# Where half range checks and one chunk's finish stand in the order of a gated-attention and SoLU kernel

## The chip, the cores and the metric

The kernel runs on one core of a Trainium2 chip. Its time is the device time of one execution in microseconds (us). Before the change three runs gave a median of 378.04 us (377.9 to 379.68). The core has five engines with a queue each: TensorE (PE, matrix products), VectorE (DVE), ScalarE (ACT), GpSimd (POOL) and SyncE (SP, which here only issues transfers). An engine works through its own queue in order; between engines there are only semaphores.

## The reference

Two blocks in a row. The first is a gated linear recurrence over 768 steps for 4 batches, 8 heads and a head width of 48; the second is a feed-forward layer on its 3072 rows of 384.

```
state = alpha[:, :, t, :, None] * state + einsum('bhd,bhe->bhde', k[:, :, t], v[:, :, t])
y[:, :, t] = einsum('bhd,bhde->bhe', q[:, :, t], state)
...
h = x @ w_in                                  # 384 -> 1024
e = exp(h - max(h));  solu = h * e / (sum(e) + 1e-9)
ln = (solu - mean(solu)) / sqrt(var(solu) + 1e-6) * g_ln
out = ln @ w_out                              # 1024 -> 384
```

The weights arrive as 64-bit floats, the rest as 32-bit.

## The kernel before

**Tiling.** Time is cut into six groups g of 128 steps; a group has the 4 batches side by side, so 512 rows at once. A chunk n = 4g + b is one batch of one group, 128 rows of the output. Attention for a group is done in closed form: products of alpha run along time (DVE scans, L204), keys and queries are scaled by them, `scores` makes key-by-query products on PE in two halves of the heads, `masked` (L289, DVE) takes the part at or before the diagonal into sT, `read_state` and `read_values` make y on PE, ACT copies y to x, and `next_state` with `decay` (L261, POOL) carries the state to the next group.

**Feed-forward.** For each group there are eight ups f, one per 128 of the 1024 hidden columns. `up_mm` (L388) makes h in one of two psum buffers. `up_act` then does three steps on two engines: exponential on ACT (L402), u = h times it on DVE (L403), and the square of u on ACT (L404). The buffer of h is free when L403 has read it. For group 0 the exponential and the square go to sT, which has four places: up f uses place f % 4. `array_sums` adds the exponentials and squares over the hidden columns on PE ("quarters", L431), in a first half at up 4 and a second half after the loop, and ACT copies them (L438). `down(n, half)` (L499) multiplies u by four of the eight blocks of w_out for one chunk. `finish(n)` (L524 to L541) brings a chunk to its end: three small DVE operations, a centring one for group 0 (L533), a power on POOL (L538), a scaling on ACT (L540) and the store on SP. `hold` (L508) copies a chunk out of psum, for chunks 0 and 1.

**Weights.** The 64-bit weights come in eight pieces, 0 to 3 of w_in and 4 to 7 of w_out. `fetch` brings a piece (or two) to a slot of `room`. `bits(i, part)` converts it on DVE: part 0 is L599 and L602, part 1 is L607, L610 and L611, and without a part it does both. `in_range(i)` checks on ACT that the magnitudes can be held: a square with a sum (L587), then an exponential of it with a sum (L588). `scaled(i)` (L618, ACT) multiplies a piece of w_out by the gain. `mean` (L632 to L640) takes the mean over w_out's rows once all eight pieces are there.

**What sets the order.** The program's order is each engine's order (`tc.manual_schedule()`): nothing moves work about. The loop `for f in range(FC)` over group 0's eight ups is written out by hand, with conversions, checks, fetches and loads between the ups. The transfers named here are issued by SP in that same order, so one that waits holds all behind it. `ends_k` and `ends_q` are ACT copies of parts of the next group's k and q; they wait for those loads (`load_first`, issued at up 0). After the loop, group 1's keys and queries are made while group 0's downs run.

Of the kernel before, what the change touches and what calls it, by code (L numbers as in the profile page):

```python
# [9 lines left out]
FP = mybir.dt.float32  # L10
# [3 lines left out]
AF = mybir.ActivationFunctionType  # L14
ALU = mybir.AluOpType
AX = mybir.AxisListType
P = 128
# [15 lines left out]
def fast_path(ctx, tc, q, k, v, alpha, moe_w_in, moe_w_out, moe_g_ln, out):  # L33
# [12 lines left out]
    nc = tc.nc  # L46
# [15 lines left out]
    def pool(name, bufs, **kw):  # L62
        return ctx.enter_context(tc.tile_pool(name=name, bufs=bufs, **kw))
# [6 lines left out]
    one = pool("one", 1)  # L70
# [215 lines left out]
    def masked(half, batches=range(B)):  # L286
        a = masks[half]
        for b in batches:
            nc.vector.tensor_tensor(  # L289
                out=sT[:, b, half * NP : half * NP + NP], in0=a[b], in1=mask[:, None, :].to_broadcast([P, NP, P]),  # L290
                op=ALU.mult,
            )
# [25 lines left out]
    parts = []  # L318
# [58 lines left out]
    def u_of(g, f):  # L377
        return slots[((0, 5, 4), (1, 2, 3))[g % 2][f // 3]][:, T4 * (f % 3) : T4 * (f % 3) + T4]
# [12 lines left out]
            )  # L391
        d["h"] = h

    def up_act(g, f):
        d = gr[g]
        h = d["h"]
        if g:
            e, u2 = (ring.tile([P, T4], FP, name=x) for x in ("e", "u2"))
        else:
            e, u2 = (sT[:, f % 4, 4 * i : 4 * i + 4].rearrange("p b t -> p (b t)") for i in range(2))  # L400
        u = u_of(g, f)
        nc.scalar.activation(out=e, in_=h, func=AF.Exp)  # L402
        nc.vector.tensor_tensor(out=u, in0=h, in1=e, op=ALU.mult)  # L403
        nc.scalar.activation(out=u2, in_=u, func=AF.Square)  # L404
        d[f] = e, u2

# [15 lines left out]
    def array_sums(g, half):  # L422


        d = gr[g]
        if half == 0:
            d["q"] = [ps_a.tile([P, T4], FP, tag=f"a{i}", name=f"quarters{i}") for i in range(2)]
        for i in range(2):
            for f in range(4):
                r = quarter(f)  # L430
                nc.tensor.matmul(  # L431
                    d["q"][i][r], lhsT=ones[:, 0:32], rhs=d[4 * half + f][i], start=half == 0, stop=half == 1,
                    tile_position=(0, r.start), skip_group_check=True,
                )
        if half:
            d["p"] = one.tile([P, 2, T4], FP, name="p")
            for i in range(2):
                nc.scalar.copy(out=d["p"][:, i], in_=d["q"][i])  # L438
            d["unit"] = small_ones
# [53 lines left out]
    def down(n, half, part=range(HF)):  # L493
        g, b = divmod(n, B)
        d = st[n]
        if half == 0 and 0 in part:
            d["o"] = ps_o.tile([P, 512], FP, tag="o", name="o")
        for f in (half * HF + i for i in part):
            nc.tensor.matmul(  # L499
                d["o"][:, 0 : DM + 1], lhsT=u_of(g, f)[:, b * P : b * P + P], rhs=w_out[:, f], start=(f == 0),  # L500
                stop=(f == FC - 1), skip_group_check=True,
            )
# [7 lines left out]
    def finish(n):  # L510
        g, b = divmod(n, B)
        d = st[n]
        s, whole = sums[:, n], d.get("held", d["o"])
        o = whole[:, 0:DM]
        t0 = b * S + g * P
        if g == G - 1:
            o_sb = work.tile([P, DM], FP, name="o_sb")
            r = gr[g]["r"][:, b : b + 1]
            nc.vector.tensor_scalar(out=o_sb[:, 0:P], in0=o[:, 0:P], scalar1=r, scalar2=None, op0=ALU.mult)  # L519
            nc.scalar.activation(out=o_sb[:, P:DM], in_=o[:, P:DM], func=AF.Copy, scale=r)  # L520
            nc.scalar.dma_start(out=out[t0 : t0 + P, :], in_=o_sb)
            d.clear()
            return
        nc.vector.tensor_copy(out=s[:, 0:1], in_=whole[:, DM : DM + 1])  # L524
        t = small.tile([P, 1], FP, name="t")
        nc.vector.scalar_tensor_tensor(
            out=t, in0=s[:, 0:1], scalar=-1.0 / DFF, in1=s[:, 0:1], op0=ALU.mult, op1=ALU.mult
        )
        nc.vector.tensor_tensor(out=s[:, 3:4], in0=t, in1=gr[g]["s"][:, b : b + 1], op=ALU.add)  # L529
        if g == 0:  # L530

            centred = work.tile([P, DM], FP, name="o_mean")
            nc.vector.scalar_tensor_tensor(  # L533
                out=centred, in0=mean_sb, scalar=s[:, 0:1], in1=o, op0=ALU.mult, op1=ALU.add
            )
            o = centred
        r = small.tile([P, 1], FP, name="r")
        nc.gpsimd.tensor_tensor(out=r, in0=s[:, 3:4], in1=mhalf, op=ALU.pow)  # L538
        o_sb = work.tile([P, DM], FP, name="o_sb")
        nc.scalar.activation(out=o_sb, in_=o, func=AF.Copy, scale=r)  # L540
        nc.sync.dma_start(out=out[t0 : t0 + P, :], in_=o_sb)  # L541
        d.clear()
# [8 lines left out]
    F = 2 * DM  # L551
# [5 lines left out]
    raws = {}  # L557
# [19 lines left out]
    far = const.tile([P, len(pieces), 2], FP, name="far")  # L577
    made = {}

    def in_range(i):  # L580


        if not float64:
            return
        hi = raws[i][:, :, :, 1].bitcast(FP)
        sq = one.tile([P, F], FP, name="sq").rearrange("p (c f) -> p c f", c=hi.shape[1])
        nc.scalar.activation(out=sq, in_=hi, func=AF.Square, accum_out=far[:, i, 0:1])  # L587
        nc.scalar.activation(out=sq, in_=sq, func=AF.Exp, scale=-(2.0**24), accum_out=far[:, i, 1:2])  # L588

    def bits(i, part=None):  # L590
        if not float64:
            return
        lo, hi = raws[i][:, :, :, 0], raws[i][:, :, :, 1]
        if part != 1:
            made[i] = [
                lots[2 * (i % 2) + x].rearrange("p (c f) -> p c f", c=hi.shape[1]) for x in range(2)
            ]
            top = made[i][0].bitcast(U32)
            nc.vector.tensor_scalar(  # L599
                out=top, in0=hi, scalar1=3, scalar2=0x3FFFFFF8, op0=ALU.logical_shift_left, op1=ALU.bitwise_and  # L600
            )
            nc.vector.scalar_tensor_tensor(  # L602
                out=top, in0=hi, scalar=0xC0000000, in1=top, op0=ALU.bitwise_and, op1=ALU.bitwise_or
            )
        if part != 0:
            top, low = made.pop(i)
            nc.vector.tensor_scalar(  # L607
                out=low.bitcast(U32), in0=top.bitcast(U32), scalar1=0xFF800000, scalar2=None, op0=ALU.bitwise_and
            )
            nc.vector.scalar_tensor_tensor(out=low, in0=lo, scalar=2.0**-52, in1=low, op0=ALU.mult, op1=ALU.mult)  # L610
            nc.vector.tensor_tensor(out=place(i), in0=low, in1=top, op=ALU.add)  # L611

    def scaled(i):

        f = pieces[i][1]
        for c in range(f, f + 2):
            w = w_out[:, c, 0:DM]
            nc.scalar.mul(out=w, in_=w, mul=g_col[:, c : c + 1])  # L618
# [78 lines left out]
    for i in (0, 2, 1):  # L697
        if i == 1:
# [3 lines left out]
            out=qe[:, :, 0:P] if i == 2 else qv[:, part, 0:P], in0=t[i], in1=aT[:, part, 1:SW], op=ALU.mult  # L702
# [17 lines left out]
    for f in range(FC):  # L720
        up_mm(0, f)
        if f == 4:
            array_sums(0, 0)
        up_act(0, f)

        for half in (0, 1) if f == 0 else (f + 1,):
            bits(2 + half // 2, half % 2)
        if f == 0:
            next_state(0)
            fetch(4, 3)  # L730
            load_first(k, kn, 1)
            load_first(q, qn, 1)
            load(alpha, an, 1)
        elif f == 1:
            in_range(2)
        elif f == 2:
            ends_k = ends_of(kn, "e")
        elif f == 3:
            in_range(3)
            fetch(5, 1)  # L740
            fetch(6, 2)
            ends_q = ends_of(qn, "u2")
        elif f == 5:
            in_range(4)
            fetch(7, 3)
            load_v(1)
        elif f == 6:
            scaled(4)
        elif f == 7:
            scaled(5)  # L750
    bits(6, 1)
    tk = three("tp_k", [(ps_a, "a2"), (ps_a, "a3"), (ps_h, "h")])
    turned(kn, ends_k, tk)
    load(k, kn, 2)
    array_sums(0, 1)
    down(0, 0)
    scaled(6)
    bits(7)
# [37 lines left out]
    scores(1, 0)  # L796
    decay(1)
    masked(0)
    finish(0)
    alpha_T(2)  # L800
    down(2, 1)
    scores(1, 1)
    masked(1)
    finish(1)
    finish(2)
    down(3, 0)
# [94 lines left out]
    for g in range(1, G + 1):  # L901
# [10 lines left out]
        for s in range(FC):  # L912
# [16 lines left out]
            if todo:  # L929
                n, half = todo.pop(0)  # L930
# [18 lines left out]
    parts = [N * 3, G * 2, G * NB] + [len(pieces)] * 2  # L949
# [5 lines left out]
    def compare(out, x, bound, op):  # L955
# [6 lines left out]
        out=chunks[:, :, 2], in0=sums[:, :, 2], scalar=0.25, in1=sums[:, :, 3], op0=ALU.mult, op1=ALU.is_le  # L962
# [6 lines left out]
    else:  # L969
# [9 lines left out]
        out=bad, in0=all_ok[0:1, 0:1], scalar1=float(P * ends[-1]), scalar2=None, op0=ALU.is_lt  # L979
# [451 lines left out]
```

## Time and profile before

| | |
|---|---|
| median of 3 runs | 378.04 us |
| the profiled execution's own time | 378.17 us |
| its span, first to last instruction | 376.4 us |
| PE busy | 362.0 us (96%) |
| DVE busy | 247.5 us (66%) |
| ACT busy | 145.8 us (39%) |
| POOL busy | 122.2 us (32%) |
| granted TensorE clock | 1.000 |

The profile is one execution. A timeline line gives the start and the length in us, the engine, the line of the kernel, the operation, what is written from what, the tile's shape and how many instructions were merged into it (an fp32 product of PE counts as two); in brackets stands how long the engine was idle before it and what ended that. Starts are from the span's first instruction. The span is shorter than the execution's time by what lies around it.

### The profile page before, as it was taken

The numbers are of one execution on the slowest core, as the hardware profiler recorded it, in microseconds if no ns is written. First come the engines' busy times: TensorE is split into PE (matmuls) and PEld (weight loads), VectorE is DVE, ScalarE is ACT, GpSimd is POOL, SyncE is SP. The second block draws the span as 40 slices with busy tenths as digits, with TensorE's granted clock in tenths as the row PEclk, the third lists the DMA queues.
The fourth block names the chain that finished last, engine by engine and source line by source line (L and its number), as shares of the span: only waits on it lengthen the run. The fifth ranks groups of instructions, "written<-read, shape, count | busy, mean of one in ns | idle before, by whom it ended". The sixth has DMA issues, their size and how long they took to land. (4 is left out here: it accounts for less than half of the span.)

```text
span 376.4 us, 10028 instructions
## 1 busy us (share of the span) xinstructions
PE 362.0 (96%) x4341; PEld 214.9 (57%) x4341; DVE 247.5 (66%) x377; ACT 145.8 (39%) x258; POOL 122.2 (32%) x127
## 2 busy tenths in 40 slices
PE   8989899999999999999999999999999999999994
PEld 7775335656655665556565556575556565555652
DVE  1999878997989979855756954756955314544500
ACT  3628566680365353352432351532241241332101
POOL 7000000000357992665112664112683211333200
PEclk9999999999999999999999999999999999999999
DMA  9983968239249616645034454004051000000011
GB/s 181 177 331 96 213 199 210 44 86 189 74 96 198 154 30 130 124 114 127 23 85 94 97 123 116 24 3 107 3 121 34 23 23 0 23 22 21 25 44 50
DMA packets 72439, 36.06 MB, mean 96 GB/s; under 512 B 48184, under 2 KB 69952, under 8 KB 72384
## 3 DMA queue, kind: packets, MB, share of 16 engines
q1 hardware_dynamic: 71360, 34.39, 38.8%
q10 hardware_dynamic: 1024, 0.92, 0.7%
q8 instruction: 36, 0.59, 0.7%
q14 instruction: 19, 0.16, 0.1%
HBM read 25.30 MB, written 4.72 MB: 80 GB/s over the span
## 5 line engine op out<-in xcount | busy, mean ns | idle before, releaser
L388 PE MATMUL h<-x,w_in 128*128 128x512 f32 x288 | 133.1, 601 | 3.1 <-DVE room L403 1.7
L499 PE MATMUL o<-w_out,room 128*128 128x385 f32 x384 | 133.6, 492 | 0.0
L499 PEld LDWEIGHTS o<-w_out,room 128*128 128x128 f32 x384 | 71.2, 190 | 54.5 <-issue 13.8
L388 PEld LDWEIGHTS h<-x,w_in 128*128 128x128 f32 x288 | 52.6, 190 | 61.9 <-issue 47.9
L403 DVE TENSOR_TENSOR room<-h,e 128x512 f32<-128x512 f32 x40 | 27.6, 690 | 60.8 <-ACT e L402 60.8
L402 ACT ACTIVATE e<-h 128x512 f32<-128x512 f32 x40 | 23.8, 596 | 95.2 <-PE h L388 92.6
L419 POOL TENSOR_TENSOR p<-p,e 128x512 f32<-128x512 f32 x30 | 42.9, 1429 | 27.3 <-ACT e L402 27.0
L404 ACT ACTIVATE u<-room 128x512 f32<-128x512 f32 x40 | 25.2, 630 | 36.5 <-DVE room L403 36.5
L538 POOL TENSOR_TENSOR r<-sums,mhalf 128x1 f32<-128x1 f32 x20 | 12.2, 610 | 73.7 <-DVE sums L529 73.6
L289 DVE TENSOR_TENSOR sT<-a,mask 128x512 f32<-128x512 f32 x44 | 27.3, 682 | 13.2 <-PE a L278 13.2
L419 DVE TENSOR_TENSOR p<-p,u 128x512 f32<-128x512 f32 x30 | 24.4, 814 | 7.2 <-ACT u L404 7.2
L204 DVE TENSOR_TENSOR_SCAN hT<-aT,unit 128x516 f32<-128x516 f32 x18 | 23.7, 1359 | 7.7 <-ACT aT L683 7.7
L204 DVE TENSOR_TENSOR_SCAN aT<-aT,seed 128x516 f32<-128x516 f32 x18 | 27.8, 1577 | 0.2
L212 POOL COPY fend<-hT 128x12 f32<-128x12 f32 x6 | 4.0, 667 | 67.5 <-DVE hT L204 67.5
L278 PEld LDWEIGHTS a<-qv,kT 32*128 32x128 f32 x704 | 21.2, 187 | 7.5 <-POOL r L538 1.6
L278 PE MATMUL a<-qv,kT 32*128 32x128 f32 x704 | 23.8, 278 | 0.8 <-DVE qv L793 0.6
L327 PE MATMUL y<-sT,vn 128*32 128x128 f32 x768 | 23.2, 274 | 1.3 <-DVE sT L289 0.7
L327 PEld LDWEIGHTS y<-sT,vn 128*32 128x32 f32 x768 | 20.8, 110 | 4.9 <-issue 3.8
L225 POOL TENSOR_TENSOR kT<-kT,hT 128x1024 f32<-128x1024 f32 (+1 forms) x8 | 14.2, 1795 | 20.1 <-DVE kT L179 20.1
L196 ACT ACTIVATE sq<-an,mone 128x1536 uint8<-128x1536 f32 x12 | 18.9, 1575 | 0.2
L540 ACT ACTIVATE o_sb<-o,r 128x384 f32<-128x384 f32 x16 | 9.3, 580 | 24.1 <-POOL r L538 24.1
L357 ACT COPY x<-y 128x384 f32<-128x384 f32 x24 | 11.2, 478 | 11.9 <-PE y L327 11.7
(145 smaller groups left out, 364.4 us busy)
## 6 DMA issues: line engine op xcount, KB each, us to landing
vn<-in_v_dram SPq DMA_DIRECT2D x24, 192.0 KB, 4.6
an<-in_alpha_dram SPq DMA_DIRECT2D x20, 192.0 KB, 4.2
out_dram<-o_sb SPq DMA_DIRECT2D x20, 192.0 KB, 1.9
room<-in_moe_w_in_dram SPq DMA_DIRECT2D x6, 512.0 KB, 8.3
room<-in_moe_w_out_dram SPq DMA_DIRECT2D x8, 384.0 KB, 3.9
kn<-in_k_dram SPq DMA_DIRECT2D x16, 192.0 KB, 4.5
qn<-in_q_dram SPq DMA_DIRECT2D x16, 192.0 KB, 4.5
lot<-qe SPq DMA_DIRECT2D x40, 64.5 KB, 2.1
```

The source lines that it names most:

```text
L196: nc.scalar.activation(out=sq, in_=x, func=AF.Relu, scale=sign, bias=mone, accum_out=over[:, g, i : i + 1])
L204: nc.vector.tensor_tensor_scan(out=o, data0=a, data1=s, initial=1.0, op0=ALU.mult, op1=ALU.add)
L225: nc.gpsimd.tensor_tensor(out=kT[:, part], in0=kT[:, part], in1=hk[:, part], op=ALU.mult)
L278: nc.tensor.matmul(a[b][:, i], lhsT=kT[quarter(b), kb], rhs=qv[quarter(b), qb, 0:P], start=not last and not i, stop=bool(last), tile_posit ...
L289: nc.vector.tensor_tensor(out=sT[:, b, half * NP : half * NP + NP], in0=a[b], in1=mask[:, None, :].to_broadcast([P, NP, P]), op=ALU.mult,)
L327: nc.tensor.matmul(y_bank(b)[quarter(r), a], lhsT=lhsT, rhs=rhs, start=(b, r) not in begun, stop=stop, tile_position=(row, 32 * r), skip_g ...
L388: nc.tensor.matmul(h, lhsT=w_in[:, a, f * P : (f + 1) * P], rhs=d["x"][:, a].rearrange("p b t -> p (b t)"), start=(a == 0), stop=(a == KC ...
L402: nc.scalar.activation(out=e, in_=h, func=AF.Exp)
L403: nc.vector.tensor_tensor(out=u, in0=h, in1=e, op=ALU.mult)
L404: nc.scalar.activation(out=u2, in_=u, func=AF.Square)
L419: eng.tensor_tensor(out=p, in0=d[0][i] if f == 1 else p, in1=d[f][i], op=ALU.add)
L499: nc.tensor.matmul(d["o"][:, 0 : DM + 1], lhsT=u_of(g, f)[:, b * P : b * P + P], rhs=w_out[:, f], start=(f == 0), stop=(f == FC - 1), skip ...
```

## The change

Two edits, with the same instructions before and after.

In group 0's loop, `in_range(i)` is cut into its square (part 0) and its exponential (part 1), and `up_act` takes a function that it calls between its own multiply and square. Ups 0 to 5 run the six halves of pieces 2, 3 and 4 there; before, ups 1, 3 and 5 ran both halves behind the up's square. Conversions go from "both halves of piece 2 at up 0, then half a piece an up" to half a piece an up from up 0 on, so each half comes one up later, and the whole of piece 6 comes after the loop. `scaled(5)` moves from up 7 to behind the second half of the sums.

Later, `finish(0)` moves from behind `masked(0)` to behind `masked(1)`, past `alpha_T(2)`, the second half of `down(2)`, the second `scores` and `masked(1)`.

```diff
-    def up_act(g, f):
+    def up_act(g, f, between=None):
...
         nc.vector.tensor_tensor(out=u, in0=h, in1=e, op=ALU.mult)
+        if between:
+            between()
         nc.scalar.activation(out=u2, in_=u, func=AF.Square)
...
-    def in_range(i):
+    def in_range(i, parts=(0, 1)):
...
+        if 0 in parts:
+            hi = raws[i][:, :, :, 1].bitcast(FP)
+            squares[i] = one.tile([P, F], FP, name="sq").rearrange("p (c f) -> p c f", c=hi.shape[1])
+            nc.scalar.activation(out=squares[i], in_=hi, func=AF.Square, accum_out=far[:, i, 0:1])
+        if 1 in parts:
+            sq = squares.pop(i)
+            nc.scalar.activation(out=sq, in_=sq, func=AF.Exp, scale=-(2.0**24), accum_out=far[:, i, 1:2])
...
-        up_act(0, f)
-
-        for half in (0, 1) if f == 0 else (f + 1,):
-            bits(2 + half // 2, half % 2)
+        up_act(0, f, (lambda: in_range(2 + f // 2, (f % 2,))) if f < 6 else None)
+
+        bits(2 + f // 2, f % 2)
...
-        elif f == 1:
-            in_range(2)
...
-            in_range(3)
...
-            in_range(4)
...
-        elif f == 7:
-            scaled(5)
-    bits(6, 1)
+    bits(6)
...
     array_sums(0, 1)
+    scaled(5)
     down(0, 0)
...
     masked(0)
-    finish(0)
     alpha_T(2)
     down(2, 1)
     scores(1, 1)
     masked(1)
+    finish(0)
     finish(1)
     finish(2)
```

More of the change, by code (lines that the diff above doesn't have):

```diff
@@ L578, in fast_path @@
     made = {}
-    def in_range(i):
+    squares = {}
+    def in_range(i, parts=(0, 1)):
         if not float64:
             return
[L585 to L588, printed above, removed]
+        if 0 in parts:
[5 more added lines that the diff above has]
+            nc.scalar.activation(out=sq, in_=sq, func=AF.Exp, scale=-(2.0**24), accum_out=far[:, i, 1:2])
     def bits(i, part=None):
```

## The prediction

> **What bounds the kernel now.** I read the busy shares first, then the table of 10 us windows, then TensorE's timeline for its gaps, and last the timelines of the engines named in those gaps.
>
> ```profile
> PE 362.0 (96%) x4341; PEld 214.9 (57%) x4341; DVE 247.5 (66%) x377; ACT 145.8 (39%) x258; POOL 122.2 (32%) x127
> ...
> 40.00:50.00 10.00, 8.70 (x31) 3.28 (x32) 7.28 (x10) 7.38 (x15) 0.00 (x0) 1.00 1.05 198
> ```
>
> The second column of a window is its length, the third PE's busy time. PE is busy 96% of the span; it fills every window from 100 to 370 us but two (9.74 and 9.40 from 130 to 150), so only what happens before 100 us can move the end, and it moves it by the delay with which PE leaves that part. PE's gaps there:
>
> ```profile
> 40.40 2.84 PE L388 MATMUL h<-x,w_in 128*128 128x512 f32 x6 [0.59 <-DVE room L403]
> 44.14 2.84 PE L388 MATMUL h<-x,w_in 128*128 128x512 f32 x6 [0.89 <-DVE room L403]
> 54.55 2.84 PE L388 MATMUL h<-x,w_in 128*128 128x512 f32 x6 [0.21 <-DVE room L403]
> 85.19 2.06 PE L278 MATMUL a<-qv,kT 32*128 32x128 f32 x62 [0.60 <-DVE qv L793]
> 95.43 1.82 PE L327 MATMUL y<-lot,state 64*32 64x128 f32 x64 [0.60 <-POOL state L261]
> ```
>
> The first three lie in the loop of ups: h of up f+2 needs the psum buffer that the multiply L403 of up f frees. The last two decide. At 85.19 PE waits for DVE's second L793, the end of a DVE row without a gap since 69.31; at 95.43 for the decay of the state on POOL, which waits for transfers queued behind the load of alpha at 80.03, itself behind ACT's alpha_over. Both rows start when the conversion of the last weight piece ends on DVE (its last L611). DVE before that:
>
> ```profile
> 43.39 0.69 DVE L403 TENSOR_TENSOR room<-h,sT 128x512 f32<-128x512 f32 x1 [1.19 <-ACT sT L402]
> 50.75 0.69 DVE L403 TENSOR_TENSOR room<-h,sT 128x512 f32<-128x512 f32 x1 [2.14 <-ACT sT L402]
> 57.55 0.69 DVE L403 TENSOR_TENSOR room<-h,sT 128x512 f32<-128x512 f32 x1 [1.60 <-ACT sT L402]
> 68.43 0.96 DVE L611 TENSOR_TENSOR w_out<-lot 128x768 f32<-128x768 f32 x1
> 84.45 0.69 DVE L793 TENSOR_TENSOR qv<-tp_q,aT 128x512 f32<-128x512 f32 x1
> ```
>
> DVE stood 1.19+2.14+1.60 = 4.93 us for ACT's exponential, since on ACT a whole range check lies ahead of it:
>
> ```profile
> 40.92 0.90 ACT L587 ACTIVATE sq<-room 128x768 f32<-128x768 f32 x1
> 41.72 0.19 ACT L587 ACTIVATION_READ_ACCUMULATOR sq<-room 128x1 f32 x1
> 41.94 0.84 ACT L588 ACTIVATE sq<-sq 128x768 f32<-128x768 f32 x1
> 42.69 0.19 ACT L588 ACTIVATION_READ_ACCUMULATOR sq<-sq 128x1 f32 x1
> 42.78 0.58 ACT L402 ACTIVATE sT<-h 128x512 f32<-128x512 f32 x1
> 44.12 0.63 ACT L404 ACTIVATE sT<-room 128x512 f32<-128x512 f32 x1 [0.76 <-DVE room L403]
> ```
>
> **Halved range checks and conversions.** Nothing is added or removed; work changes place. From start to next start, on ACT: exponential 0.51, square 0.54, first half of a check 0.90, second 0.84, an ends copy 0.51, a scaled piece 1.01; on DVE: multiply 0.61, first half of a conversion 0.98+0.88 (w_in) or 0.59+0.88 (w_out), second half 0.59+0.99+0.88; on PE 2.71 an up (34.40 to 39.82 for two), a quarter sum 1.93. A half check goes into the hole of 0.76 in which each square waits for its multiply, so the square starts 0.1 to 0.2 later and nothing waits for it. If the hole were gone it would cost its whole 0.9. With these steps the loop of before comes out at 69.33 for the last L611 against 69.39 measured. The new order:
>
> - Up 0 as before (exponential 34.01, multiply 34.62); DVE is free at 37.09, since half of piece 2 is left for later. Multiply 1 runs at 37.90 (exponential 37.28) in place of 39.67: h 3 starts without its 0.59.
> - Exponential 2 follows h 2 at 39.99 in place of 42.78; multiply 2 at 40.97, when DVE has done piece 2. h 4 starts at 42.53; its 0.89 is gone, and piece 2, which it reads, is ready at 41.1.
> - ends_k reaches ACT at 42.2. k's two loads are issued at 34.5 and 35.0 and take 7.2 us at most, so they are in. Exponential 3 at 42.73, multiply 3 at 43.44.
> - ends_q reaches ACT at 44.7, ahead of q: issued at 40.4, 5.1 to landing, 45.5. ACT stands 0.8, and exponential 4 queues behind. It can't run before 46.3 anyway: it overwrites sT that the first quarter sums read until 1.05 after 45.24. Multiply 4 at 46.94. q could land 1.9 later at no cost, as DVE then stands 1.64 for h 5: exponential 5 at 50.05, multiply 5 at 50.66.
> - Multiply 6 at 53.73, behind DVE. scaled(4) holds exponential 7 to 55.99, multiply 7 at 56.61; then three halves more than before: pieces 5 (half), 6 and 7 take 11.2. Last L611 ends at 67.84.
>
> DVE's waits are now 0.80+0.43+1.64+0.80 = 3.67. **Gain at the last L611: 69.39-67.84 = 1.55.** PE itself is 2 us early after the loop and 3.1 at down(0,0) (59.9 against 63.00), as the quarter sums no longer wait for square 7. scaled(5), now behind the two copies of the sums on ACT, ends at 61.7, when down(0,0) needs it: 0 to 0.3, paid from those 3.1. PE then stands in mean(0) for scaled(7) and at the scores for L793, so 1.5 of the 3.1 is all that passes.
>
> SP's queue: the fetches of pieces 5 and 6 wait for piece 3's L610, now 45.6 (48.77 before), the fetch of piece 7 and v behind it some 3 us earlier; none of these was waited for, so nothing. After the last L611 ACT does scaled(7), two checks, o_mean (1.55 earlier); mean(1) on PE started at 75.03 with PE's own previous work and now with o_mean, 0.1 sooner. So alpha's load, and the eight qe and four qv transfers behind it on SP, move by 1.6, and the decay starts at 92.9 in place of 94.54.
>
> **finish(0) behind masked(1).** Four DVE operations (89.50 to 90.48: 0.98) leave the way of alpha_T(2) and masked(1). masked(1) ended 95.74 while read_values, its reader, starts at 100.03: no gain. alpha_T(2) comes at 88.0, and alpha's loads, now issued from 78.4 to 79.8 with 4.8 to landing, are in. Queued behind finish(0): finish(1), (2) and the scans on DVE, the power on POOL, o_sb on ACT, the store on SP. The power waited for the decay before it on POOL (96.14) anyway.
>
> But finish(0) now meets the decay. DVE reaches it at 93.2 (95.67 for finish(1) less 1.5 less 0.98), and its L526 at 93.3 falls in the decay's first half (92.9 to 93.7). The trace has such meetings:
>
> ```profile
> 94.54 1.64 POOL L261 TENSOR_TENSOR state<-state,lot 128x384 f32<-128x384 f32 x2 [15.53 <-DMA lot<-qv]
> ...
> 95.83 0.36 DVE L526 SCALAR_TENSOR_TENSOR t<-sums 128x1 f32<-128x1 f32 x1
> ...
> 97.02 0.16 DVE L526 SCALAR_TENSOR_TENSOR t<-sums 128x1 f32<-128x1 f32 x1
> ...
> 126.19 1.50 DVE L419 TENSOR_TENSOR p<-p,u 128x512 f32<-128x512 f32 x1
> ```
>
> L526 takes 0.16, and 0.36 where it met the decay's end; L419 0.66 alone and 1.50 against POOL. The Trainium skill (SBUF — State Buffer, "Who interferes with whom") says more: the port pair that DVE and GpSimd share is locked by one instruction at a time, and the loser stands until it is free. By the rows alone DVE pays and PE nothing: gain 1.6. By the rule L526 waits for the first half to end, may go in ahead of the second half (0.1 to 0.2), or, were it L533's turn, hold it for 0.61; and PE needs the second half at once. I take 0.15 (L526 is the one that stands there); ends 0 and 0.6. DVE itself comes some 1.0 late to the scans, which costs nothing: the next multiply L403 (109.20) may be 2.4 late before h waits for it at 112.31.
>
> **Sum.** 1.6 - 0.15 = 1.45. The profiled execution took 378.17 (span 376.4 and 1.8 around it): 376.7. Its own time lies 0.13 above the median of the runs, so 376.6 against 378.04, -0.4%.
>
> **Rivals.**
> 1. More passes: if PE's 3.1 us lead got through because the row behind L611 shortens too. For it: nothing but the lead; against it: DVE's row 69.31 to 84.45 has no gap to close. 375.5 (2.5 gained).
> 2. Little passes: the decay is held. DVE keeps the port through finish(0) and (1) (93.3 to 95.0), and the second half ends 1.3 late; or the transfers from 80.03 on don't start earlier. 377.7.
> 3. Slower: ends_q stops ACT. It stands in front of exponential 4 and thus of multiply 4 and h 6. Free to a landing of q at 47.4, then 1 us for 1; from 48.9 on it eats the gain, and at 51 the time is 380. Against: q landed at 45.5, and the loads ahead of it on SP are not moved.
> 4. No effect: the checks are in the hole but DVE is full anyway (9.76 of 10 in the window from 70 to 80). Against: its 4.93 of waits in the loop. 378.0.
>
> **How the numbers follow.** Main case 0.60, its own range 376.1 to 377.1 (lock 0 to 0.6, steps 0.3); rival 1 0.14, rivals 2 and 4 0.16, rival 3 0.10. The range 375.6 to 378.1 leaves out the slower case and the rest of rival 1. About 0.5%, 1.9 us, is what a measurement of this kernel can tell from no change; faster by that, under 376.15: rival 1 and a fifth of the main case, 0.26. Slower 0.09, the rest 0.65.
>
> **What would show it.** Right: h 3, h 4 and h 7 with no wait on L403, four DVE waits of 0.4 to 1.7 at multiplies 1, 4, 5, 7, the last L611 ending near 67.8, scores near 83.6 still waiting for L793, the decay near 93 with finish(0) against it. Wrong: the last L611 not before 69, an exponential 4 behind a late q, a gap of 0.3 or more ahead of down(0,0)'s later matmuls, or the decay's second half much longer than 0.84.

## The result, and the profile after the change

| | before | after |
|---|---|---|
| median of 5 runs each, taken together (us) | 378.1 (377.9 to 379.68) | 376.35 (375.64 to 377.28) |
| ratio of the times | | 0.9943 [0.9926, 0.9959] |
| profiled execution: time, span (us) | 378.17, 376.4 | 377.28, 375.5 |
| TensorE busy (us) | 362.0 | 361.2 |
| last conversion L611, now L618, ends, after h 0's first product (us) | 39.23 | 37.30 |
| the scores' wait on TensorE ends, likewise | 55.04 | 52.97 |
| read_state's wait on TensorE ends, likewise | 65.28 | 63.17 |
| second decay on GpSimd starts, likewise | 99.38 | 98.45 |
| last TensorE work ends, likewise | 341.29 | 340.53 |

The changed kernel is 0.57% faster; 376.6 had been forecast. Since executions differ by some tenths in when the first h starts (30.16 before, 29.90 after), all moments that are compared below count from the start of the first product of h 0. The profiled execution of the changed kernel was the slowest of its five runs, which matters below.

First the busy shares and the windows of 10 us of the kernel after (length, TensorE's busy time, then TensorE's weight loads and the other engines):

```profile
PE 361.2 (96%) x4341; PEld 215.5 (57%) x4341; DVE 247.9 (66%) x377; ACT 145.9 (39%) x258; POOL 121.9 (32%) x127
...
40.00:50.00 10.00, 10.00 (x35) 3.77 (x35) 8.41 (x12) 7.42 (x16) 0.00 (x0) 1.00 1.17 242
...
130.00:140.00 10.00, 8.90 (x247) 6.43 (x248) 6.52 (x6) 4.24 (x8) 9.86 (x11) 1.00 0.19 41
```

The loop's window, 8.70 before, is full. The window from 130 got worse (9.74 before); the one behind it, 9.40 before, is full. TensorE's timeline has the detail:

```profile
34.14 10.57 PE L388 MATMUL h<-x,w_in 128*128 128x512 f32 x24
46.49 7.99 PE L388 MATMUL h<-x,w_in 128*128 128x512 f32 x18
...
58.89 2.88 PE L501 MATMUL o<-w_out,room 128*128 128x385 f32 x8
...
82.86 2.06 PE L278 MATMUL a<-qv,kT 32*128 32x128 f32 x62 [0.52 <-DVE qv L794]
...
93.07 1.82 PE L327 MATMUL y<-lot,state 64*32 64x128 f32 x64 [0.57 <-POOL state L261]
...
130.49 1.02 PE L327 MATMUL y<-lot,state 64*32 64x128 f32 x48 [0.70 <-POOL state L261]
```

Before, h 3, h 4 and h 7 each stood for a multiply L403. Now four ups run in one row (x24: three products an up, each counted as two), and the row after it starts at 44.64; three follow from 46.49, and the next row starts at 54.41; no row of the loop has a wait ahead of it. The two waits that decide, at the scores and at read_state, are still there, and come sooner. At 130.49 stands a new one of 0.70, for the second decay.

VectorE after, in its timeline:

```profile
37.65 0.69 DVE L403 TENSOR_TENSOR room<-h,sT 128x512 f32<-128x512 f32 x1 [0.86 <-ACT sT L402]
43.42 0.69 DVE L403 TENSOR_TENSOR room<-h,sT 128x512 f32<-128x512 f32 x1 [0.17 <-ACT sT L402]
47.17 0.69 DVE L403 TENSOR_TENSOR room<-h,sT 128x512 f32<-128x512 f32 x1 [0.60 <-ACT sT L402]
50.00 0.69 DVE L403 TENSOR_TENSOR room<-h,sT 128x512 f32<-128x512 f32 x1 [0.68 <-ACT sT L402]
55.93 0.69 DVE L403 TENSOR_TENSOR room<-h,sT 128x512 f32<-128x512 f32 x1 [0.73 <-ACT sT L402]
66.24 0.96 DVE L618 TENSOR_TENSOR w_out<-lot 128x768 f32<-128x768 f32 x1
```

VectorE's waits for an exponential are 0.86 + 0.17 + 0.60 + 0.68 + 0.73 = 3.04 where they were 4.93, and the last conversion ends at 67.20. Counted from h 0 that is 1.93 sooner.

### The profile page after: what moved, and what is told of

Its sections match the earlier page's. It is cut to its first block, busy times and chain, and to the rows that moved or that the text cites. A ratio compares the mean times of both kernels' runs of the same rounds, so it can differ in the third digit from the quotient of the medians.

```text
span 375.5 us, 10028 instructions
## 1 busy us (share of the span) xinstructions
PE 361.2 (96%) x4341; PEld 215.5 (57%) x4341; DVE 247.9 (66%) x377; ACT 145.9 (39%) x258; POOL 121.9 (32%) x127
## 5 line engine op out<-in xcount | busy, mean ns | idle before, releaser
L403 DVE TENSOR_TENSOR room<-h,e 128x512 f32<-128x512 f32 x40 | 27.7, 693 | 61.9 <-ACT e L402 61.9
L421 POOL TENSOR_TENSOR p<-p,e 128x512 f32<-128x512 f32 x30 | 41.5, 1383 | 27.7 <-ACT e L402 27.4
L421 DVE TENSOR_TENSOR p<-p,u 128x512 f32<-128x512 f32 x30 | 24.3, 811 | 7.2 <-ACT u L406 7.2
```

What stands on the lines that cost most here:

```text
L421: eng.tensor_tensor(out=p, in0=d[0][i] if f == 1 else p, in1=d[f][i], op=ALU.add)
```

## The experiments

The two parts of the change came first, then the two halves of its first part: the checks and the conversions. A second set asked what limits the gain, a third took the best form further. Each ratio is against the kernel before on the same chip. In the first set its runs scattered (median 378.51 of 28 runs, 376.95 to 381.0), in the second its median was 378.14 of 12 runs, in the third 378.7 of 10.

### Each part alone

finish(0) moved, nothing else (before, edited):

```diff
     masked(0)
-    finish(0)
     alpha_T(2)
     down(2, 1)
     scores(1, 1)
     masked(1)
+    finish(0)
     finish(1)
```

> The kernel before with finish(0) alone moved behind masked(1). Theory (the gain comes out of the loop, finish(0) lies off TensorE's path): the same time as before, ratio 0.998 to 1.002; the decay's second half stays at 0.84 us and starts where it did (94 to 95 us), DVE stands in finish(0)'s two-source operations. Rival A (the later finish carries part of the gain, since masked(1) comes 1 us sooner): 0.5 to 1 us faster. Rival B (the port lock holds the decay): 0.2 to 0.6 us slower, decay's second half longer than 1 us.

Measured: 378.25, ratio 0.9982 [0.9958, 1.0006]. No effect that this resolves; the interval reaches from 1.6 us faster to 0.2 slower. In the trace the decay's halves keep their 0.84, so rival B is out, and the scores' wait ends 54.98 after h 0 (55.04 before), read_state's 65.02 (65.28).

The loop changed, finish(0) where it was (the change, with that step put back):

```diff
     masked(0)
+    finish(0)
     alpha_T(2)
     ...
     masked(1)
-    finish(0)
     finish(1)
```

> The changed kernel with finish(0) put back in front of alpha_T(2). Theory: as the changed kernel, 1.5 to 2.2 us faster than before, the last conversion ends near 67.2 us. Rival A: 0.5 to 1 us of the gain is lost.

Measured: 376.5, ratio 0.9930 [0.9901, 0.9960]. The gain is the loop's; the move of finish(0) neither adds to it nor takes from it beyond the intervals, and by the trace the last conversion (37.28 after h 0) and the scores (52.90) come as with the full change.

Of the loop, the checks alone (before, with only the halves of the range checks put between exponential and square; conversions, scaled(5) and finish(0) as before):

```diff
-        up_act(0, f)
+        up_act(0, f, (lambda: in_range(2 + f // 2, (f % 2,))) if f < 6 else None)
         for half in (0, 1) if f == 0 else (f + 1,):
             bits(2 + half // 2, half % 2)
...
-            in_range(2)
...
-            in_range(3)
...
-            in_range(4)
```

> The kernel before with the range checks alone cut in two and put between exponential and square; conversions, scaled(5) and finish(0) as before. From the recurrence of the prediction with TensorE's step set to 2.64 us as measured in the changed kernel: DVE waits only 1.4 us in the loop (in place of 4.9 before and 3.4 changed), since the half conversion that the change puts off is done at up 0; last conversion ends near 65.6 (67.2 changed, 69.4 before), scores start near 81.8; 2.5 to 3.2 us faster than before, so faster than the changed kernel by about 1. It may lose TensorE waits of 0.7 ahead of h 3. Rival (the checks and the half conversions are both needed, since DVE stays in front of multiply 1): 0 to 1 us faster than before.

Measured: 377.08, ratio 0.9953 [0.9922, 0.9984]. The last conversion did come early: 35.57 after h 0, against 39.23 before and 37.30 with the full change. Of the 2.5 to 3.2 us expected of that, only 1.4 came. In this kernel's timeline of TensorE:

```profile
72.23 0.81 PE L646 MATMUL sums<-o_mean,ones 128*128 128x384 f32 x2
...
75.84 1.93 PE L164 MATMUL tp_q<-ident,u 128*32 128x128 f32 x32 [2.80 <-DVE kT L773]
```

TensorE stands 2.80 us ahead of the turns of q, for the multiply that reads the third block of turned keys. In the kernel before (and, as long, in the change) the same row waits for ScalarE's copy of the mean instead:

```profile
76.41 1.08 PE L164 MATMUL tp_q<-ident,u 128*32 128x128 f32 x32 [0.57 <-ACT mean_sb L640]
```

The tile that these turns write, tp_q2, is taken from the same psum pool of two banks as that block. With the steps in this order it seems to have got that block's bank, and in the two other kernels the one that the mean had used: that is read from what ended the waits, since the trace names no banks, and why the banks came out otherwise isn't settled. So VectorE's lead was lost again at a wait that neither the kernel before nor the change has.

The conversions alone (before, with half a conversion an up and scaled(5) behind the sums; whole checks as before):

```diff
-        for half in (0, 1) if f == 0 else (f + 1,):
-            bits(2 + half // 2, half % 2)
+        bits(2 + f // 2, f % 2)
...
-        elif f == 7:
-            scaled(5)
-    bits(6, 1)
+    bits(6)
...
     array_sums(0, 1)
+    scaled(5)
```

> The kernel before with the conversions alone moved to half a piece an up from up 0 on, scaled(5) behind the sums; whole range checks behind the square at ups 1, 3 and 5 and finish(0) as before. Recurrence: DVE waits 0.75+0.66+1.2+0.7+0.8 = 4.0 us, last conversion ends near 68.2; 1.0 to 1.4 us faster than before. Rival (checks alone make the gain): same as before or up to 1 us slower, because the work put off comes back behind the loop.

Measured: 377.65, ratio 0.9969 [0.9946, 0.9993]; last conversion 38.26 after h 0, scores 53.87 (before: 55.04). The time gained, 0.86 by the medians, is a little under the 1.0 to 1.4 expected. Leaving half a conversion for later helps a little where whole checks stand in ScalarE's way, since VectorE then has work left to do in its waits. The two halves don't add up: the last conversion comes 3.66 sooner by checks alone, 0.97 by conversions alone, 1.93 by both. VectorE's waits in the loop say the same: 4.93 before, 1.36 with the checks alone (0.24 + 0.41 for exponentials, 0.71 for a transfer of w_out), 3.99 with the conversions alone, 3.04 with both.

### What limits the gain

The checks alone, with tp_q2 taken from the other psum pool (one line on top of the kernel with the checks alone):

```diff
-    tq += three("tp_q2", [(ps_h, "h")])
+    tq += three("tp_q2", [(ps_o, "o")])
```

> The run of the halved checks alone, with the third block of turned queries (tp_q2) in a psum bank of the o pool in place of the h pool, so that it doesn't stand 2.80 us for the third key multiply, which held the bank that it had been given. Theory (halved checks are the part that pays, half conversions put work off, and only that bank hid it): last conversion ends 35.6 us after h 0 as in that run, the scores' second wait ends 51.5 to 52.2 after h 0 (52.97 in the changed kernel, 54.48 in the run of checks alone), the first decay starts 61.0 to 61.7 after h 0; 2.3 to 3.2 us faster than before, 0.4 to 1.2 faster than the changed kernel. Rival (DVE's earlier end meets another wait of 1 us or more before the scores): scores not before 53 after h 0, no faster than the changed kernel.

Measured: 375.37, ratio 0.9927 [0.9911, 0.9944]; once more in the third set 375.27, ratio 0.9904 [0.9884, 0.9924] (375.0 to 375.8 had been expected of that). The first one's timeline of TensorE:

```profile
73.77 1.08 PE L164 MATMUL tp_q<-ident,u 128*32 128x128 f32 x32 [0.95 <-ACT lot L510]
...
81.47 2.19 PE L278 MATMUL a<-qv,kT 32*128 32x128 f32 x64
92.49 1.81 PE L327 MATMUL y<-lot,state 64*32 64x128 f32 x64 [1.25 <-POOL state L261]
```

The wait of 2.80 is gone, and so is the one ahead of the scores, which reach the product that waited elsewhere 51.42 after h 0 (53.87 to 55.04 in the kernels with whole checks, 54.48 with the checks alone, 52.97 with the change). That settles, by the trace, what became of the lead that the checks alone gave VectorE: it had been lost at the wait for that pool's tile. By time it is less plain: the ratio's interval overlaps that of the checks alone in the first set, and the change itself in the same set (376.0, below) is 0.63 slower by the medians, with single runs of 375.56 to 376.23 against 375.2 to 375.76, while the intervals of the two ratios overlap. What is left now stands at read_state: 1.25 for the decay, which hangs on the transfers, not on VectorE's row.

scaled(4) one up later (the change, edited):

```diff
-        elif f == 6:
+        elif f == 7:
             scaled(4)
```

> The changed kernel with scaled(4) put behind up 7 in place of up 6, so that exponential 7 follows h 7 at once. Theory (the row from the last conversion on sets the pass to the scores, so each wait of DVE in the loop is worth its length): DVE's wait ahead of multiply 7 falls from 0.73 to under 0.2, last conversion and the scores each 0.5 to 0.7 sooner after h 0 than in the changed kernel (37.30 and 52.97), time 0.3 to 0.7 under it. Rival (something else holds the scores): last conversion sooner, scores unchanged.

Measured: 375.33, ratio 0.9923 [0.9906, 0.9940]. The change itself in the same set, below, gave 376.0 and 0.9941 [0.9925, 0.9958]: 0.67 slower by the medians, with intervals that overlap. The trace tells the two apart: VectorE's wait ahead of multiply 7 is gone, its last conversion ends 36.49 after h 0 (37.30 and 37.27 in the two profiled executions of the change) and the scores' wait 52.19 after it (52.97 and 52.92).

TensorE loaded with 1.28 us of idle products behind the loop (the change, with a row of products added whose output nobody reads):

```diff
     bits(6)
+    warm(5)
     tk = three("tp_k", [(ps_a, "a2"), (ps_a, "a3"), (ps_h, "h")])
```

> The changed kernel with five more 128x128 products (some 1.2 us of TensorE work whose output nobody reads) between the loop and the turning of the keys. Theory (TensorE's lead behind the loop is not what passes): down(0,0) starts 1.2 later after h 0 (28.99 in the changed kernel), its wait of 0.59 in mean(0) goes, scores unchanged within 0.2 (52.97), time as the changed kernel within 0.5. Rival (the lead passes): scores and time 1.2 later.

Measured: 376.32, ratio 0.9953 [0.9936, 0.9970]. Its timeline of TensorE:

```profile
54.57 1.28 PE L446 MATMUL warm<-ones 128*128 128x128 f32 x10
...
60.26 2.88 PE L501 MATMUL o<-w_out,room 128*128 128x385 f32 x8
...
83.13 2.06 PE L278 MATMUL a<-qv,kT 32*128 32x128 f32 x62 [0.51 <-DVE qv L795]
```

down(0,0), the row at 60.26, starts 1.1 later after h 0 than without the load (30.10 against 28.99). The wait of 0.59 that the change has in mean(0), at 67.62, is gone, and the scores wait just as long for VectorE and are done waiting 52.98 after h 0, as without the load. So TensorE's lead behind the loop isn't what passes through.

The change itself once more, in that set:

> The changed kernel once more, beside the three above. Every theory: 1.4 to 2.2 us faster than before. For the point why its first profile kept only 1.0 of the 2.3 us that TensorE led at read_state: if the transfers of group 2 (alpha, k, v, then the two sets for the decay) vary from execution to execution, the second decay's start after h 0 lies between 96.5 and 98.5, and the end follows it; if the change itself slows them, it is near 98.4 again.

Measured: 376.0, ratio 0.9941 [0.9925, 0.9958]. The last conversion, the scores and read_state come within 0.05 of the first profile (37.27, 52.92, 63.12 after h 0). The second decay comes at 97.48 in place of 98.45 and the last work on TensorE at 339.37 in place of 340.53. The same kernel thus differs by about 1 us in what follows read_state. (The 2.3 of the expectation is 95.43 less 93.07, from the span's start; from h 0 it is the 2.11 of the table.)

### A version that is faster than both

The remaining wait at read_state hangs on SyncE's queue: alpha's load, with the transfers of qe and qv behind it, is issued only once ScalarE has done alpha_over, behind two range checks. Taking those two checks behind it is the next step (the kernel with the checks alone and the other bank, edited):

```diff
-    in_range(5)
-    in_range(6)
+    alpha_over(1)
+    load(alpha, an, 2)
     ...
-    alpha_over(1)
-    load(alpha, an, 2)
     ...
+    in_range(5)
+    in_range(6)
     in_range(7)
```

> The run of halved checks with tp_q2 in the other bank, and with alpha_over(1) and alpha's load in the place of the checks of pieces 5 and 6, which go to the check of piece 7 at the scores. Theory (after the loop's gain the read of the state waits for the decay, whose transfers queue behind alpha's load): alpha's load is issued at 71 to 73 us in place of 77.0, the decay starts before TensorE reaches read_state, the wait of 1.25 us there falls under 0.3; 0.8 to 1.3 faster than the same kernel without it, 374.0 to 374.6. Rival (the transfers wait for qe and qv made on DVE, or the next gate takes it back): no faster than it.

Measured: 373.71 (373.09 to 374.8), ratio 0.9867 [0.9847, 0.9888]. The load of alpha on SyncE's queue stood at 77.00 in the first profile of the other-bank kernel,

```profile
77.00 1.79 SPq L134 DMA_DIRECT2D an<-in_alpha_dram  x4
```

and in this version at 69.89, with the decay on GpSimd 57.82 after h 0 rather than 61.40. TensorE's timeline of this version:

```profile
90.86 0.40 PE L327 MATMUL y<-lot,state 64*32 64x128 f32 x2
91.49 1.52 PE L327 MATMUL y<-lot,state 64*32 64x128 f32 x62 [0.22 <-DVE sT L289]
```

read_state no longer waits for the decay; two of its products run ahead, and the rest stand 0.22 for VectorE. The wait of 1.25 for the decay has become one of 0.22 for another engine. The end comes at 338.27 after h 0, against 338.62 and 339.13 in the two profiled executions without this step; in the same set the median was 373.71 against 375.27, and the intervals of the two ratios overlap by 0.0004. The 1.56 between the medians is more than the 0.86 between the profiled ends in that set, because the profiled execution of this version, 374.8, was the slowest of its six. Against the change (0.9941 [0.9925, 0.9958], in another set) the gain is clear of the intervals.

## Why the prediction was right, and where its sizes were off

**The bound and the path held.** TensorE's gaps ahead of 100 us were what could move; h 3, h 4 and h 7 lost theirs, and the two rows that start at the last conversion carried the gain on. It was 1.93 there, 2.07 at the scores and 2.11 at read_state, each after h 0. Predicted were 1.55, 1.5 and 1.6 less 0.15. TensorE's own lead at down(0,0) was 3.85 (28.99 after h 0, 32.84 before), and as forecast only the part that VectorE's row let through reached the scores. That row was 0.14 shorter as well (15.00 from 67.12 to 82.12, 15.14 from 69.31 to 84.45), for a reason that no run here shows.

**The mis-sized term of the loop is TensorE's step.** The prediction took 2.71 for an up, half the length of this row of before:

```profile
34.40 5.42 PE L388 MATMUL h<-x,w_in 128*128 128x512 f32 x12
```

No wait lies in that row; its two ups start and end as the first two of the longer row after, within 0.01. But a row's length holds something once that doesn't come again with each up. Rows of one, two, three and four ups take 2.84, 5.42, 7.99 and 10.57, so one more up costs 2.57 or 2.58. From start to the next row's start an up is 2.63 (44.64 less 34.14, over four) or 2.64 (54.41 less 46.49, over three). Exponential 5 waits for h 5, behind four ups and the first quarter sums. The ups took 10.50 for 10.84, the sums 1.85 (46.49 less 44.64) for 1.93: 0.42 in all. Multiply 5 starts 20.10 after h 0 (50.00 less 29.90), forecast was 20.50 (50.66 less 30.16), and these 0.40 are all of what the last conversion gained beyond the forecast (37.30 against 37.68 after h 0). That the prediction's steps gave the loop of before to 0.06 did not test this one: there only exponential 1 waits for an h. VectorE's waits, forecast at 3.67, came to 3.04. The largest of them, 1.64 for h 5, was 0.68: multiply 4 came 0.49 later than forecast (17.27 rather than 16.78 after h 0), because q's landing had been put too early, and h 5 came 0.40 earlier.

**ends_q stood for q, at no cost.** ScalarE's timeline of the kernel after:

```profile
39.59 0.60 ACT L402 ACTIVATE sT<-h 128x512 f32<-128x512 f32 x1 [0.59 <-PE h L388]
40.09 0.91 ACT L592 ACTIVATE sq<-room 128x768 f32<-128x768 f32 x1
41.43 0.63 ACT L406 ACTIVATE sT<-room 128x512 f32<-128x512 f32 x1 [0.34 <-DVE room L403]
42.27 0.62 ACT L155 COPY e<-kn 128x512 f32<-128x512 f32 x1 [0.21 <-DMA kn<-in_k_dram]
...
46.02 0.62 ACT L155 COPY u<-qn 128x512 f32<-128x512 f32 x1 [1.24 <-DMA qn<-in_q_dram]
46.54 0.59 ACT L402 ACTIVATE sT<-h 128x512 f32<-128x512 f32 x1
```

The half check at 40.09 lies between exponential and square, and the square still stands 0.34 for its multiply: the hole takes the half check, as forecast. ends_q begins at 46.02, which is 16.12 after h 0 where 15.34 was forecast, so it stood 1.24 rather than 0.8. That is a misreading of before, not an effect of the change: q's two loads take 5.1 and 5.6 from issue to landing in both profiles, and the prediction put 5.1 on the later one, issued at 40.4, so q was not in at 45.5 before either. ends_k stood 0.21 for k, which had been thought to be in. Both are hidden, because VectorE still stands 0.68 for h 5 one multiply later. Of the reserve of 1.9 q's 0.78 and the 0.40 of h 5 are used up, and 0.68 is about what remains: rival 3 didn't come, but its cover is thin. In the repeat of the change ends_q stood 1.51 and VectorE 0.38 for h 5, with scaled(4) later 1.95 and 0.19.

**scaled(5)** cost nothing: down(0,0) takes 2.88 in one row, 2.86 before.

**finish(0) and the lock.** It was put at 0.15, with ends of 0 and 0.6. In the first part of finish(0), VectorE after shows

```profile
92.51 0.52 DVE L528 SCALAR_TENSOR_TENSOR t<-sums 128x1 f32<-128x1 f32 x1
93.07 0.77 DVE L531 TENSOR_TENSOR sums<-t,s 128x1 f32<-128x1 f32 x1
...
94.46 0.16 DVE L528 SCALAR_TENSOR_TENSOR t<-sums 128x1 f32<-128x1 f32 x1
```

and GpSimd after

```profile
92.18 1.64 POOL L261 TENSOR_TENSOR state<-state,lot 128x384 f32<-128x384 f32 x2 [15.50 <-DMA lot<-qv]
93.92 2.51 POOL L540 TENSOR_TENSOR r<-sums,mhalf 128x1 f32<-128x1 f32 x3
```

L528 ends at 93.03 and L531 at 93.84; the decay's halves end at about 93.02 and 93.82 (0.84 each from 92.18, and 0.84 to 0.86 for this decay in every profile of these runs). So each of the two stood until a half was over, and L528 took 0.16 once the decay was done. The two halves took 1.64 together, exactly as before. That agrees with the rule of the Trainium skill (SBUF — State Buffer, "Who interferes with whom") that the loser stands until the port pair is free, but the decay was not the loser at this meeting: each half had begun before the VectorE operation that it kept waiting. The term is 0, not 0.15. That agrees with finish(0) alone making no difference; its interval is too wide to show a cost of 0.15 by itself.

**Less of the 2.11 was kept in the profiled execution.** Its second decay came only 0.93 sooner after h 0, and the end 0.76. A hole of 0.42 inside read_state's products, at 97.88, is the first part (0.17 in the repeat). The next is SyncE's queue, which feeds the second decay: the second group's load of alpha was issued at 105.99, 1.66 sooner after h 0 than before (107.91), but k's load behind it took longer to issue, here before and after,

```profile
109.84 2.85 SPq L134 DMA_DIRECT2D kn<-in_k_dram  x4
107.92 3.48 SPq L134 DMA_DIRECT2D kn<-in_k_dram  x4
```

and the qv transfers ended their issue at 126.85, only 0.97 sooner. So GpSimd came late, and then its second decay took longer too. GpSimd and VectorE after:

```profile
128.35 2.09 POOL L261 TENSOR_TENSOR state<-state,lot 128x384 f32<-128x384 f32 x2 [1.45 <-DMA lot<-qv]
128.74 0.99 DVE L421 TENSOR_TENSOR p<-p,u 128x512 f32<-128x512 f32 x1
```

Both halves took 2.09 in place of 1.64: the second one, from 129.15 to 130.44, took 1.29. VectorE's L421 had begun 0.41 ahead of it and was at work until 129.74. This time it was GpSimd that stood, for 0.45, and that is most of the 0.70 that TensorE stands at 130.49. In the repeat of the same kernel k's load took 2.99, the second decay was at 97.48 and took 1.65, L421 began behind it and took 1.14, and 1.92 of the gain was still there at the end (341.29 less 339.37). That this part varies between executions is shown by the repeat; why the issue of k's load varies is not settled.

The time came out at 376.35 for 376.6: 0.5 to 0.7 more gain up to read_state than forecast, part of it not kept in the profiled execution. Two errors of opposite sign lie behind a difference of 0.25, so that closeness is in part luck; in the repeat, in the second set, the gain was 2.14 by the medians for a forecast of 1.45.

**The rivals.** Rival 1, that TensorE's own lead passes, fell with the added load: 1.28 us in TensorE's way left the scores where they were. Rivals 2 and 4 fell by the trace: the decay came sooner and kept its 0.84, and VectorE's waits did shrink. Rival 3 had its cover cut to 0.68 but didn't bite. What no rival named is that the second half of the change, half a conversion an up, works against the first: with the checks alone the last conversion came 1.73 sooner than with both (35.57 against 37.30). It reached the scores only with tp_q2 from the other pool (51.42 against 52.97), where the median was 0.63 lower than the change's; that gain in time is small beside the intervals.

## What to carry to other kernels

Take an engine's step from the difference between two rows' lengths, or from one start to the next; the length of a row over the number of its steps carries a part that comes once (2.71 for 2.63 here), and the error grows with each step. Take a landing from the transfer that lands last, not from the shortest of them. Filling a hole in one engine's row helps only as far as the next engine has nothing of its own to do there, so try each half of a paired change alone, and look at the gate behind it: here the gains came at a psum bank, then at a decay that hung on a load behind two range checks. When steps change order, see what each psum tile now waits for, because a bank that is read late can eat most of a gain.

## What the runs showed of the hardware

- At the two meetings of VectorE and GpSimd that were followed here, the one that had begun first kept its time. At finish(0) the decay's halves kept their 0.84 and VectorE's operations on a single column grew from 0.16 to 0.52 and 0.77; at the second decay VectorE's L421 had begun 0.41 ahead of GpSimd's second half, and that half grew from 0.84 to 1.29. Of the three powers on GpSimd just after finish(0)'s meeting, from 93.92, one took 0.55 and two 0.86, with VectorE at work beside them; whether that is the same lock wasn't tried.
- Two executions of the same kernel reached read_state 0.05 us apart and the second decay 1 us apart (98.45 and 97.48 after h 0). A difference of under 1 us in this part of one trace is no finding.
